# Attention scores as plain float32 products, two heads in turn on halves of the rows, in a banded attention with a GLU behind it

## The chip, the core and the metric

The kernel runs on one core of a Trainium2 chip. The metric is the device time of one execution in microseconds: the median of 3 runs before is 849.68 us (849.67 to 851.6). The engines are TensorE (PE in the rows; PEld is its weight load), VectorE (DVE), ScalarE (ACT), GpSimd (POOL) and SyncE (SP), which issues all DMAs here.

## The reference

There are 8 batches of 8 heads, 512 local tokens, 32 global tokens, head size 64. A local query sees the 32 global keys and the local keys at most 32 places away; a global query sees all 544 keys.

```python
k_all, v_all = concat(k_g, k_l), concat(v_g, v_l)
out_g = softmax(q_g @ k_all.T / 8) @ v_all
s_ll = where(|i - j| <= 32, q_l @ k_l.T / 8, -1e9)
out_l = softmax(concat(q_l @ k_g.T / 8, s_ll)) @ v_all
x = concat(out_g, out_l)                  # 4608 tokens x 512 (8 heads x 64)
out = ((x @ w1) * (x @ w2)) @ w3 @ w_out  # d_model 512, d_ff 1024
```

## The kernel before

Heads are taken one after the other (n = 0 to 63), the two heads of a pair (m = n // 2) share tiles. For each head the scores of a block of 128 queries against their window of keys (192 or 256 columns: 32 global keys and the band, `WIN`) are made by PE into the tile `s`, which has one buffer of two banks. DVE then scales, masks and takes the row's largest value in one pass per block (`minus_max`, line 550), written to one of two tiles P; ACT takes the exponential with its sum (line 554); PE transposes P (line 583), ACT and DVE copy that into the tiles PT and G, some edges go through DRAM (`gd`, `G<-gd`), and PE multiplies with the values (`av`, lines 659 and 665). Pairs are normalized with a reciprocal that goes through DRAM (`rd`, `R`). The 32 global queries have their own scores (`sg`), in the same buffer `s`.

The GLU is folded: w34 = w3 @ w_out is made on the chip in float32 (`fold`, line 950) while the weights arrive. Then every 256 tokens are multiplied with w1 and w2 (`first`, lines 816 to 818, tiles ap and bp), gated, and multiplied with w34 (`second`, lines 848 to 850, acc). These products are of type float32r: each operand is split into a high part of that type and the rest (low), and three products (high x high, high x low, low x high) are added.

Two ways of making scores stand side by side. Heads 0 to 15 (n < `NS`) use plain float32: one load of K and one of Q per pair, with the two heads on the partitions 0 to 63 and 64 to 127, and four products per head on that half of the rows (line 539); the trace has two records for each plain float32 product. Heads 16 to 63 use the split: K is loaded twice, on both halves, ACT rounds it to the high part (`kh`), POOL or DVE subtract (`kl`); Q becomes one tile with the high part on 64 partitions and the low part on the other 64 (`qs`); eight products per head on all 128 rows (line 546).

The order of the whole program is made before it runs. Each step has a cost per engine (`COST`) and a due number from the table `DUE`; `list_schedule` goes through simulated time, and on each free engine the ready step with the lowest due number begins. `take` and `read` add the waits for tiles with few buffers. All engines then run their steps in that fixed order. Seven `idle_products` open the program on PE: three on all rows, then four in turn on rows 0 to 63 and 64 to 127 (lines 390 to 396), on zeros.

Of the kernel before, what the change touches and what calls it, by code (L numbers as in the profile page):

```python
# [7 lines left out]
F32 = mybir.dt.float32  # L8
# [12 lines left out]
KD = 608  # L21
# [9 lines left out]
def i(ap):  # L31
# [3 lines left out]
NX, NO, NK, NQ, MA, NS = (5, 6), 3, 3, 2, 4, 16  # L35
# [10 lines left out]
    scores32=1650, values32=(1180, 1130), gscores32=930, take=(446, 521),  # L46
# [272 lines left out]
def band_attention_glu_kernel(  # L319
# [35 lines left out]


    cs = const.tile([128, 128 + 256 + 192], F32, tag="cs", name="cs")
    ident = cs[:, 0:128]
    mask = cs[:, 128:384]
    masks = [cs[:, 384:576], mask, mask, mask[:, 0:192]]  # L360
    Ps = [const.tile([128, PW], F32, tag=f"P{e}", name=f"P{e}") for e in range(2)]
    TT = const.tile([128, 2, 352], F32R, tag="TT", name="TT")
    vgs = const.tile([128, H, 2, 64], F32R, tag="vgs", name="vgs")
    xg = const.tile([128, NP, TG], F32, tag="xg", name="xg")
    sums = p1q.tile([128, 2, 2, 4], F32, tag="sums", name="sums")

    def view(ap, offset, *dims):
# [1109 lines left out]
```

## Time and profile before

| | us |
|---|---|
| median of 3 runs | 849.68 |
| span of the profiled execution | 848.0 |
| TensorE busy | 833.2 (98%) |
| VectorE busy | 567.0 (67%) |
| ScalarE busy | 536.0 (63%) |
| GpSimd busy | 383.4 (45%) |

The span runs from the first to the last instruction; launch and end lie outside it. Products on PE are pipelined: a row's duration is that of one record, and the next one may start before it ends, so what a product costs a busy PE is read from start to start.

### The profile page before, as it was taken

What the parts mean: (1) busy time and instruction counts of PE and PEld (TensorE: products, weight loads), DVE (VectorE), ACT (ScalarE), POOL (GpSimd) and SP (SyncE); (2) the same over time, 40 slices, a digit from 0 to 9 for tenths busy, and PEclk for the clock granted to TensorE, in tenths of its full rate; (3) what the DMA queues carried; (4) which work ended last, traced back from release to release, by engine and by line L of the source; (5) the groups of instructions that cost most, each with busy time, mean ns of one, the idle gap of its engine ahead of it and who ended that gap; (6) DMA issues with size and microseconds to landing.
All of it is one profiled execution on the core that took longest, in us unless ns stands there. A gap on an engine that the chain in (4) does not pass through costs nothing.

```text
span 848.0 us, 17752 instructions
## 1 busy us (share of the span) xinstructions
PE 833.2 (98%) x5818; PEld 750.2 (88%) x5818; DVE 567.0 (67%) x1499; ACT 536.0 (63%) x1445; POOL 383.4 (45%) x477
## 2 busy tenths in 40 slices
PE   7999999899999999999999999999999999999998
PEld 4756679799999999999999999999989999999997
DVE  5677777867777786877787767776877778531111
ACT  4666776765767786867666768676767767521111
POOL 1201455534638474747563645654755656310000
PEclk8999999999999999999999999999999999999999
DMA  9787656554647464746554554645555644200000
GB/s 292 228 250 229 183 165 165 144 129 104 147 94 170 114 158 109 170 104 165 114 137 118 131 142 121 140 116 143 123 136 123 146 97 117 50 26 2 26 18 33
DMA packets 194372, 109.75 MB, mean 129 GB/s; under 512 B 150056, under 2 KB 158504, under 8 KB 194280
## 3 DMA queue, kind: packets, MB, share of 16 engines
q1 hardware_dynamic: 194280, 108.61, 50.1%
q8 instruction: 46, 0.75, 0.4%
q14 instruction: 46, 0.38, 0.2%
HBM read 85.52 MB, written 20.28 MB: 125 GB/s over the span
## 4 chain that ended last, share of the span: by engine, by line
PE 75%; DMA 3%; SPq 1%; ACT 0%; issue 0%; POOL 0%; DVE 0%; ACTq 0%; POOLq 0%
PE acc L848 7%; PE acc L849 7%; PE ap L816 7%; PE acc L850 7%; PE bp L816 7%; PE bp L817 6%; PE ap L817 6%; PE bp L818 6%; PE ap L818 6%; PE av L665 5%; PE s L546 5%; PE t L583 3%; DMA G<-gd 2%; PE av L659 2%; PE sg L715 1%; PE s L539 1%
## 5 line engine op out<-in xcount | busy, mean ns | idle before, releaser
L816 PE MATMUL ap<-x,w12h 128*128 128x256 f32 x544 | 153.8, 283 | 0.0
L816 PE MATMUL bp<-x,w12h 128*128 128x256 f32 x544 | 153.0, 281 | 0.0
L817 PE MATMUL bp<-x,w12h 128*128 128x256 f32 x544 | 151.1, 278 | 0.0
L817 PE MATMUL ap<-x,w12h 128*128 128x256 f32 x544 | 151.0, 278 | 0.0
L818 PE MATMUL bp<-x,w12l 128*128 128x256 f32 x544 | 151.0, 278 | 0.0
L818 PE MATMUL ap<-x,w12l 128*128 128x256 f32 x544 | 150.9, 277 | 0.0
L554 ACT ACTIVATE P<-P,small 128x256 f32<-128x256 f32 (+1 forms) x256 | 121.5, 476 | 19.0 <-DVE small L550 18.7
L550 DVE CUSTOM_DVE_ANT_0 P<-s,cs 128x192 f32<-128x192 f32 (+1 forms) x256 | 88.3, 383 | 25.8 <-PE s L546 16.5
L816 PEld LDWEIGHTS ap<-x,w12h 128*128 128x128 f32 x544 | 102.3, 188 | 2.1 <-issue 0.4
L817 PEld LDWEIGHTS bp<-x,w12h 128*128 128x128 f32 x544 | 102.5, 188 | 1.1
L817 PEld LDWEIGHTS ap<-x,w12h 128*128 128x128 f32 x544 | 102.5, 188 | 1.1
L816 PEld LDWEIGHTS bp<-x,w12h 128*128 128x128 f32 x544 | 102.2, 188 | 1.4 <-issue 0.2
L818 PEld LDWEIGHTS bp<-x,w12l 128*128 128x128 f32 x544 | 102.6, 189 | 0.0
L818 PEld LDWEIGHTS ap<-x,w12l 128*128 128x128 f32 x544 | 102.4, 188 | 0.0
L679 DVE TENSOR_TENSOR u<-av,cb 64x352 f32<-64x352 f32 x112 | 57.5, 519 | 27.1 <-ACT cb L462 25.2
L465 POOL TENSOR_TENSOR kl<-kr,kh 128x608 fp32r<-128x608 f32 x37 | 56.5, 1527 | 36.9 <-ACT kh L462 26.6
L665 PE MATMUL av<-PT,vs 128*128 128x192 f32 x448 | 61.4, 263 | 0.0
L950 PE MATMUL w<-wo,w3f 128*128 128x512 f32 x128 | 60.2, 604 | 0.0
L462 ACT COPY cb<-av 64x352 f32<-64x352 f32 x93 | 41.6, 447 | 27.2 <-PE av L665 25.9
L665 PEld LDWEIGHTS av<-PT,vs 128*128 128x128 f32 x448 | 52.4, 162 | 0.7
L465 POOL TENSOR_TENSOR qs<-qr,qs 64x512 fp32r<-64x512 f32 x31 | 42.4, 1368 | 17.6 <-issue 9.3
L554 ACT ACTIVATION_READ_ACCUMULATOR P<-P,small 128x1 f32 x256 | 48.1, 188 | 0.0
(811 smaller groups left out, 2137.9 us busy)
## 6 DMA issues: line engine op xcount, KB each, us to landing
kr<-in_kd_t_dram SPq DMA_DIRECT2D x96, 152.0 KB, 3.0
raw_w<-in_w_t_dram SPq DMA_DIRECT2D x24, 512.0 KB, 4.9
kpr<-in_kp_t_dram SPq DMA_DIRECT2D x32, 272.0 KB, 3.2
out_dram<-o_None SPq DMA_DIRECT2D x33, 256.0 KB, 2.8
R<-rd SPq DMA_DIRECT2D x64, 128.0 KB, 3.2
gd<-TT SPq DMA_DIRECT2D x112, 64.0 KB, 2.7
vr<-in_v_t_dram SPq DMA_DIRECT2D x28, 256.0 KB, 3.2
G<-gd SPq DMA_DIRECT2D x112, 64.0 KB, 2.7
```

The source lines that it names most:

```text
L465: (eng or nc.gpsimd).tensor_sub(dst, src, f(hi))
L550: nc.vector.tensor_tensor_reduce(blk(n, e), T["st", n][:, e, 0 : WIN[e][1]], masks[e], -0.125, 3.0e38, ALU.add, ALU.min, T["mn", n][:, e : ...
L554: nc.scalar.activation(blk(n, e), blk(n, e), AF.Exp, bias=T["mn", n][:, e : e + 1], scale=-1.0, accum_out=T["sm", n // 2][:, n % 2, e : e ...
L665: nc.tensor.matmul(av[0:r, o : o + 32 * (s1 - s0)], v[:, 0:r], PT[:, s0:s1, y, j], start=False, stop=(j % 2 == 1 and (plain or y == 1)), s ...
L679: nc.vector.tensor_add(T["u", n // 2][r : r + 64, x], T.pop(("av", n, x))[r : r + 64, 0:352], T["cb", n][r : r + 64, x])
L816: nc.tensor.matmul(d, wh[:, k, c, :], x[:, 0, 0:w], start=(k == m % 2 == 0), stop=False, skip_group_check=True)
L817: nc.tensor.matmul(d, wh[:, k, c, :], x[:, 1, 0:w], start=False, stop=False, skip_group_check=True)
L818: nc.tensor.matmul(d, wl[:, k, c, :], x[:, 0, 0:w], start=False, stop=(k == 3), skip_group_check=True)
L848: nc.tensor.matmul(a, gh[:, m % 2, sl], wh[:, c], start=(m == 0), stop=False, **part)
L849: nc.tensor.matmul(a, gh[:, m % 2, sl], wl[:, c], start=False, stop=False, **part)
L850: nc.tensor.matmul(a, gl[:, m % 2, sl], wh[:, c], start=False, stop=(m in (5, 7)), **part)
L950: nc.tensor.matmul(T["w34", t], T["w3f", t, j // 4][:, j % 4], T["wo"][:, j], start=(j == 0), stop=(j == 7))
```

## The change

All 64 heads get their scores as plain float32 products. `scores(m, h)` makes half of the windows (e = 0, 1 or e = 2, 3) for both heads of a pair, the heads in turn, head 0 on rows 0 to 63 into one bank and head 1 on rows 64 to 127 into the other; so there are 64 score steps of four products with a planned cost of 872 ns instead of 16 of four with 1650 ns and 48 of eight with 897 ns. The split of K and Q, its loads and its steps go. P has three tiles. The table DUE has new numbers (its first line is shown). At the end of the program 22 products on the float32r weights are added, whose results nothing reads.

```diff
-NX, NO, NK, NQ, MA, NS = (5, 6), 3, 3, 2, 4, 16
+NX, NO, NK, NQ, MA, NP_ = (5, 6), 3, 3, 2, 4, 3
-    scores32=1650, values32=(1180, 1130), gscores32=930, take=(446, 521),
+    scores2=872, values32=(1180, 1130), gscores32=930, take=(446, 521),
 DUE = tuple(int(x) / 100 for x in """
-    3500 0 102500 2500 274500 5000 273000 1500 500 7500 7000 9500 6000 19500 19000 21000 9000 27500 28000 30000 13500 36500 36000 37000
+    47500 225000 87500 1382500 163000 1058500 371500 1268000 274500 1018000 1698500 664500 297000 700500 68000 337500 313500 366500 23000 1072000 865000 1788500 737500 787000
...
-    Ps = [const.tile([128, PW], F32, tag=f"P{e}", name=f"P{e}") for e in range(2)]
+    Ps = [const.tile([128, PW], F32, tag=f"P{e}", name=f"P{e}") for e in range(NP_)]
+    def trial_products():
+        a, b = (W12[m][0].rearrange("p a b c -> p (a b c)") for m in (0, 1))
+        o = [ps_1.tile([128, 512], F32, tag=t, name=f"trial_{t}") for t in ("t0", "t1", "a", "b")]
+        def product(at, st, mv, w=256, rows=(0, 128), cols=128, out=None):
+            r = slice(*rows)
+            d = o[at][0:cols, 0:w] if out is None else out
+            nc.tensor.matmul(d, b[r, st : st + cols], mv if mv is not None else a[r, st : st + w], start=True, stop=True,
+                             skip_group_check=True)
+        for j in range(3):
+            product(0, 128 * j, None)
+        for j in range(3):
+            product(0, 128 * j, None, rows=(0, 64))
+            product(1, 128 * j, None, rows=(64, 128))
+        for j in range(3):
+            product(2, 128 * j, None, cols=64)
+        for j in range(2):
+            product(3, 128 * j, view(a, 0, [2, 256]))
+        for j in range(2):
+            for r in range(4):
+                product(r, 128 * j, None, rows=(32 * r, 32 * r + 32))
...
-    def scores(n):
...
-        qs, kh, kl = T.pop(("qs", n)), T.pop(("kh", n)), T.pop(("kl", n))
-        for e in range(4):
+    def scores(m, h):
+        st = ps_1.tile([128, 2, 2, 256], F32, tag="s", name=f"s{m}_{h}")
...
+        q, k = T["q2", m], T["k2", m]
+        for e in (2 * h, 2 * h + 1):
             o, w = WIN[e]
-            for j, kk in enumerate((kh, kl)):
-                nc.tensor.matmul(st[:, e, 0:w], qs[:, 128 * e : 128 * e + 128], kk[:, o : o + w],
-                                 start=(j == e % 2 == 0), stop=(j == 1), skip_group_check=True)
+            for x in range(2):
+                r = slice(64 * x, 64 * x + 64)
+                nc.tensor.matmul(st[:, x, e % 2, 0:w], q[r, 128 * e : 128 * e + 128], k[r, o : o + w],
+                                 start=(e % 2 == 0), stop=True, skip_group_check=True)
...
-            if n + 1 < NH:
-                take("s", 1, ("s", n + 1), ("s", n + 1))
+            if n % 2 and n + 1 < NH:
+                for k in (("s", (n + 1) // 2, h) for h in range(2)):
+                    take("s", 1, k, k)
...
+        trial_products()
```

What the order of instructions shows. First PE in the steady part: before, head 32 is scored by one block between main products (kh and kl are the parts of K, qs those of Q).

```order
L817 MATMUL ap2_1_6_4834<-x2_3_1_3798,w12h6_999 128x256
L818 MATMUL ap2_1_6_4834<-x2_3_1_3798,w12l6_1000 128x256
L546 MATMUL s32_4856<-kh32_4776,qs32_4754 128x192
L546 MATMUL s32_4856<-kl32_4788,qs32_4754 128x192
L546 MATMUL s32_4856<-kh32_4776,qs32_4754 128x256
L546 MATMUL s32_4856<-kl32_4788,qs32_4754 128x256
L546 MATMUL s32_4856<-kh32_4776,qs32_4754 128x256
L546 MATMUL s32_4856<-kl32_4788,qs32_4754 128x256
L546 MATMUL s32_4856<-kh32_4776,qs32_4754 128x192
L546 MATMUL s32_4856<-kl32_4788,qs32_4754 128x192
L816 MATMUL bp2_1_6_4872<-x2_0_1_2782,w12h6_999 128x256
L817 MATMUL bp2_1_6_4872<-x2_0_1_2782,w12h6_999 128x256
```

Now the same pair (16) has two blocks on the undivided tiles kq and qp. The first:

```order
L798 MATMUL bp2_1_4_4483<-x2_3_1_3587,w12l5_1042 128x256
L526 MATMUL s16_0_4610<-kq16_3835,qp16_4119 128x192 x2
L526 MATMUL s16_0_4610<-kq16_3835,qp16_4119 128x256 x2
L796 MATMUL ap2_1_6_4617<-x2_0_1_2704,w12h6_1043 128x256
L797 MATMUL ap2_1_6_4617<-x2_0_1_2704,w12h6_1043 128x256
L798 MATMUL ap2_1_6_4617<-x2_0_1_2704,w12l6_1044 128x256
```

Between it and the second stand 36 main products:

```order
L797 MATMUL bp2_1_6_4638<-x2_3_1_3587,w12h7_1045 128x256
L798 MATMUL bp2_1_6_4638<-x2_3_1_3587,w12l7_1046 128x256
L526 MATMUL s16_1_4675<-kq16_3835,qp16_4119 128x256 x2
L526 MATMUL s16_1_4675<-kq16_3835,qp16_4119 128x192 x2
L639 MATMUL av0_31_4681<-G1_1103,vgs_83 128x288
L645 MATMUL av0_31_4681<-PT1_1059,vs15_4462 128x192
L645 MATMUL av0_31_4681<-PT1_1059,vs15_4462 64x192
```

The eight products of one head have become four, the first half of the windows of two heads, and the second half follows 36 products later.

Next PE at the start of the program: before, one head is scored ahead of the first fold and transposes (w34 is the fold, t a transpose, sg the scores of global queries).

```order
L707 MATMUL sg0_151<-kpr0_116,QG0_112 128x272 x2
L396 MATMUL idle0_102<-vgs_82 128x256 x2
L539 MATMUL s0_170<-kq0_129,qp0_127 128x192
L539 MATMUL s0_170<-kq0_129,qp0_127 128x256 x2
L539 MATMUL s0_170<-kq0_129,qp0_127 128x192
L707 MATMUL sg1_188<-kpr1_140,QG0_112 128x272 x2
L950 MATMUL w34_0_196<-wo_99,w3f0_0_146 128x512
L583 MATMUL t0_0_201<-cs_78,P0_79 128x128 x4
L588 MATMUL t1_0_202<-cs_78,P0_79 128x128 x3
```

Now both halves of pair 0 stand there in a row:

```order
L687 MATMUL sg0_155<-kpr0_128,QG0_113 128x272 x2
L386 MATMUL idle0_103<-vgs_83 128x256 x2
L526 MATMUL s0_0_168<-kq0_115,qp0_132 128x192 x2
L526 MATMUL s0_0_168<-kq0_115,qp0_132 128x256 x2
L526 MATMUL s0_1_181<-kq0_115,qp0_132 128x256 x2
L526 MATMUL s0_1_181<-kq0_115,qp0_132 128x192 x2
L687 MATMUL sg1_206<-kpr1_140,QG0_113 128x272 x2
L930 MATMUL w34_0_216<-wo_100,w3f0_0_187 128x512
L563 MATMUL t0_0_224<-cs_78,P0_79 128x128 x4
L568 MATMUL t1_0_225<-cs_78,P0_79 128x128 x3
```

and those of pair 1 a little later, with one fold between its second half and the transposes of its first head:

```order
L930 MATMUL w34_1_236<-wo_100,w3f1_0_213 128x512
L930 MATMUL w34_0_216<-wo_100,w3f0_0_187 128x512
L526 MATMUL s1_1_351<-kq1_195,qp1_144 128x256 x2
L526 MATMUL s1_1_351<-kq1_195,qp1_144 128x192 x2
L930 MATMUL w34_0_216<-wo_100,w3f0_1_336 128x512
L563 MATMUL t0_2_375<-cs_78,P2_81 128x128 x4
L568 MATMUL t1_2_376<-cs_78,P2_81 128x128 x3
L687 MATMUL sg2_390<-kpr2_165,QG0_113 128x272 x2
```

The second half of a pair, and with it four passes on DVE, has moved ahead of the first fold; head 1 is scored there too.

Last SP, which issues the loads: before, around heads 32 and 33 (kr is K on both halves, qr is Q, gd and G the edges by way of DRAM).

```order
L401 DMA qr32_4371<-in_q_t_dram 64x512
L611 DMA gd28_4377<-TT_81 128x4x32 x2
L605 DMA PT1_1050<-TT_81 32x2x96
L606 DMA PT1_1050<-TT_81 32x2x96
L419 DMA kr32_4419<-in_kd_t_dram 64x608
L420 DMA kr32_4419<-in_kd_t_dram 64x608
L431 DMA vr15_4433<-in_v_t_dram 128x512
L616 DMA G1_1045<-gd28_4377 32x16x32 x2
L419 DMA kr33_4461<-in_kd_t_dram 64x608
L420 DMA kr33_4461<-in_kd_t_dram 64x608
```

Now, around pair 16:

```order
L415 DMA qp15_3749<-in_q_t_dram 128x512
L438 DMA kpr15_3752<-in_kp_t_dram 128x544
L545 DMA rd13_3786<-sums_85 128x2x4
L591 DMA gd26_3802<-TT_82 128x4x32 x2
L421 DMA kq16_3835<-in_kd_t_dram 128x608
L585 DMA PT1_1059<-TT_82 32x2x96
L586 DMA PT1_1059<-TT_82 32x2x96
L596 DMA G1_1103<-gd26_3802 32x16x32 x2
```

Four K loads of a pair have become one (kq), and its two Q loads one (qp); the moves into PT, gd and G have fewer issues ahead of them.

## Rows read from the trace of the kernel before

**Rows 1.** The page: busy us (share) by engine, granted clock in 40 slices.

```profile
PE 833.2 (98%) x5818; PEld 750.2 (88%) x5818; DVE 567.0 (67%) x1499; ACT 536.0 (63%) x1445; POOL 383.4 (45%) x477
PEclk8999999999999999999999999999999999999999
```

**Rows 2.** Stretches: us, busy us (xinstructions) per engine, granted clock, DMA share, GB/s.

```profile
0.00:25.00 25.00, 19.13 (x68) 13.46 (x69) 14.34 (x42) 11.20 (x31) 4.18 (x9) 0.86 0.85 275
25.00:116.00 91.00, 91.00 (x335) 55.30 (x333) 66.00 (x178) 62.71 (x172) 21.43 (x26) 1.00 0.71 216
116.00:200.00 84.00, 81.23 (x572) 74.26 (x571) 63.90 (x177) 56.85 (x167) 45.47 (x63) 1.00 0.56 145
200.00:740.00 540.00, 537.66 (x4094) 509.59 (x4093) 399.51 (x1068) 384.14 (x1040) 308.55 (x376) 1.00 0.54 127
740.00:848.00 108.00, 104.21 (x757) 97.61 (x755) 23.26 (x37) 21.06 (x39) 3.80 (x6) 1.00 0.06 21
```

**Rows 3.** Waits of PE: total us, times, longest us.

```profile
PE s L539 <- DVE small L734: 3.4, 2, 1.9
PE av L659 <- DMA G<-gd: 2.4, 6, 0.8
PE sg L707 <- DMA kpr<-in_kp_t_dram: 2.0, 1, 2.0
```

**Rows 4.** Timeline of PE at 175 us: start us, us, line, operation.

```profile
175.04 0.28 PE L818 MATMUL bp<-x,w12l 128*128 128x256 f32 x1
175.24 1.78 PE L539 MATMUL s<-kq,qp 64*128 64x192 f32 x8
176.95 0.38 PE L816 MATMUL ap<-x,w12h 128*128 128x256 f32 x1
177.17 0.28 PE L817 MATMUL ap<-x,w12h 128*128 128x256 f32 x1
```

**Rows 5.** Timeline, two narrow windows of one plain block.

```profile
193.62 0.59 PE L539 MATMUL s<-kq,qp 64*128 64x256 f32 x2
...
194.49 0.48 PE L539 MATMUL s<-kq,qp 64*128 64x192 f32 x2
```

**Rows 6.** Timeline of PE at 285 us, around a block of split scores.

```profile
284.83 0.28 PE L817 MATMUL bp<-x,w12h 128*128 128x256 f32 x1
284.95 0.28 PE L818 MATMUL bp<-x,w12l 128*128 128x256 f32 x1
...
285.96 0.30 PE L816 MATMUL ap<-x,w12h 128*128 128x256 f32 x1
286.10 0.28 PE L817 MATMUL ap<-x,w12h 128*128 128x256 f32 x1
```

**Rows 7.** PE by shape until 6.2 us: xcount | busy us, mean ns.

```profile
L396 PE MATMUL idle<-vgs 128*128 128x256 f32 x6 | 2.9, 661 | 1.2 <-DVE vgs L393 1.2
L396 PE MATMUL idle<-vgs 64*128 64x256 f32 x8 | 2.0, 643 | 0.0
```

**Rows 8.** Groups by shape, ACT and POOL: passes over K.

```profile
L462 ACT CAST kh<-kr 128x608 fp32r<-128x608 f32 x48 | 33.5, 699 | 20.5 <-PE s L546 16.8 <-issue 2.2 <-POOL QG L465 1.5
...
L465 POOL TENSOR_TENSOR kl<-kr,kh 128x608 fp32r<-128x608 f32 x37 | 56.5, 1527 | 36.9 <-ACT kh L462 26.6 <-DVE small L550 3.2 <-PE av L659 2.7
```

**Rows 9.** Group by shape, DVE: the pass that reads the scores.

```profile
L550 DVE CUSTOM_DVE_ANT_0 P<-s,cs 128x256 f32<-128x256 f32 x128 | 49.9, 418 | 0.1
```

**Rows 10.** Timeline of PE, first 16 us; in brackets idle time and its releaser.

```profile
10.38 1.78 PE L539 MATMUL s<-kq,qp 64*128 64x192 f32 x8 [1.91 <-DVE small L734]
14.15 2.15 PE L707 MATMUL sg<-kpr,QG 128*128 128x272 f32 x4 [2.00 <-DMA kpr<-in_kp_t_dram]
```

**Rows 11.** Timeline of all engines, the last 4 us.

```profile
843.94 0.28 PE L850 MATMUL acc<-w34h,gl__11088 128*128 128x256 f32 x1
844.65 0.82 SPq L863 DMA_DIRECT2D out_dram<-o  x2
```

**Rows 12.** Stretches as above, records of line 539 alone (PE, then weight loads).

```profile
116.00:200.00 84.00, 11.58 (x53) 8.77 (x51) 1.00 0.56 145
```

More of the change, by code (lines that the diff above doesn't have):

```diff
@@ L396, in idle_products @@
             nc.tensor.matmul(T["idle"][r0 // 64][:, 0:w], z[r0:r1, 0:128], z[r0:r1, 0:w], start=True, stop=True)
-    def load_q(n):
-        b, h = divmod(n, H)
-        qr = p2.tile([128, 512], F32, tag="qr", name=f"qr{n}", bufs=NQ)[0:64]
-        nc.sync.dma_start(qr, q_t[b, h])
-        T["qr", n] = qr
+    def trial_products():
[18 more added lines that the diff above has]
+                product(r, 128 * j, None, rows=(32 * r, 32 * r + 32))
     def load_q2(m):
@@ L414, in load_k2 @@
         T["k2", m] = kr
-    def load_k(n):
-        b, h = divmod(n, H)
-        kr = p2.tile([128, KD], F32, tag="kr", name=f"kr{n}", bufs=NK)
-        nc.sync.dma_start(kr[0:64], kd_t[b, h])
-        nc.sync.dma_start(kr[64:128], kd_t[b, h])
-        T["kr", n] = kr
     def load_pair(n):
@@ L482, in prep_vg @@
             lo_of(vgs[0:64, :, 1, :], vgr, vgs[0:64, :, 0, :], eng)
-    def prep_k(n, part, eng=None):
-        if part == 0:
-            T["kh", n] = p1.tile([128, KD], F32R, tag="kh", name=f"kh{n}")
-            hi_of(T["kh", n], T["kr", n], eng)
-        else:
-            T["kl", n] = p1.tile([128, KD], F32R, tag="kl", name=f"kl{n}")
-            lo_of(T["kl", n], T.pop(("kr", n)), T["kh", n], eng)
-    def prep_q(n, part, eng=None):
-        if part == 0:
-            T["qs", n] = p1q.tile([128, 512], F32R, tag="qs", name=f"qs{n}")
-            hi_of(T["qs", n][0:64], T["qr", n], eng)
-        else:
-            qs = T["qs", n]
-            lo_of(qs[64:128], T.pop(("qr", n)), qs[0:64], eng)
     def prep_v(n, s, part, eng=None):
@@ L524, in blk @@
     def blk(n, e):
-        return Ps[n % 2][:, PAT[e] : PAT[e] + WIN[e][1]]
-    def scores(n):
-        st = ps_1.tile([128, 4, 256], F32, tag="s", name=f"s{n}")
-        T["st", n] = st
-        T["mn", n] = minima()[:, 4 * (n % 2) : 4 * (n % 2) + 4]
-        if n % 2 == 0:
-            T["sm", n // 2] = sums[:, n // 2 % 2]
-        if n < NS:
-            rows = slice(64 * (n % 2), 64 * (n % 2) + 64)
-            q, k = T["q2", n // 2][rows], T["k2", n // 2][rows]
-            for e in range(4):
-                o, w = WIN[e]
-                nc.tensor.matmul(st[:, e, 0:w], q[:, 128 * e : 128 * e + 128], k[:, o : o + w], start=(e % 2 == 0),
-                                 stop=True, skip_group_check=True)
-            return
-        qs, kh, kl = T.pop(("qs", n)), T.pop(("kh", n)), T.pop(("kl", n))
-        for e in range(4):
+        return Ps[n % NP_][:, PAT[e] : PAT[e] + WIN[e][1]]
+    def scores(m, h):
+        st = ps_1.tile([128, 2, 2, 256], F32, tag="s", name=f"s{m}_{h}")
+        for x in range(2):
+            T["st", 2 * m + x] = st
+        if h == 0:
+            T["sm", m] = sums[:, m % 2]
+            for x in range(2):
+                c = 4 * ((2 * m + x) % 2)
+                T["mn", 2 * m + x] = minima()[:, c : c + 4]
+        q, k = T["q2", m], T["k2", m]
+        for e in (2 * h, 2 * h + 1):
             o, w = WIN[e]
-            for j, kk in enumerate((kh, kl)):
-                nc.tensor.matmul(st[:, e, 0:w], qs[:, 128 * e : 128 * e + 128], kk[:, o : o + w],
-                                 start=(j == e % 2 == 0), stop=(j == 1), skip_group_check=True)
+            for x in range(2):
+                r = slice(64 * x, 64 * x + 64)
+                nc.tensor.matmul(st[:, x, e % 2, 0:w], q[r, 128 * e : 128 * e + 128], k[r, o : o + w],
+                                 start=(e % 2 == 0), stop=True, skip_group_check=True)
     def minus_max(n, e):
-        nc.vector.tensor_tensor_reduce(blk(n, e), T["st", n][:, e, 0 : WIN[e][1]], masks[e], -0.125, 3.0e38,
+        nc.vector.tensor_tensor_reduce(blk(n, e), T["st", n][:, n % 2, e % 2, 0 : WIN[e][1]], masks[e], -0.125, 3.0e38,
                                        ALU.add, ALU.min, T["mn", n][:, e : e + 1])
@@ L578, in transposes @@
     def transposes(n):
-        P = Ps[n % 2]
+        P = Ps[n % NP_]
         tt = [ps_1.tile([128, 4, 128], F32, tag=f"t{x}", name=f"t{x}_{n}") for x in range(2 if n < H else 1)]
@@ L590, in turn @@
     def turn(n):
-        P, raw = Ps[n % 2][:], f(TT[:, 1])
+        P, raw = Ps[n % NP_][:], f(TT[:, 1])
         nc.vector.transpose(view(raw, 0, [128, 3], [1, 96]), view(P, 160, [32, 3], [256, 3], [1, 32]))
@@ L1013, in tile_orders @@
         take("qr", NQ, ("q2", 0, "r"), ("load", "q2", 0))
-        for k in (("sg", 0), ("s", 0), ("sg", 1), ("tg", 0)):
+        for k in (("sg", 0), ("s", 0, 0), ("s", 0, 1), ("sg", 1), ("tg", 0)):
             take("s", 1, k, k)
@@ L1019, in tile_orders @@
         for n in range(NH):
-            if n + 2 < NS and n % 2 == 0:
+            if n + 2 < NH and n % 2 == 0:
                 take("kr", NK, ("k2", n // 2 + 1, "r"), ("load", "k2", n // 2 + 1))
                 take("qr", NQ, ("q2", n // 2 + 1, "r"), ("load", "q2", n // 2 + 1))
-            if NS <= n + 2 < NH:
-                take("kr", NK, ("k", n + 2, "r"), ("load", "k", n + 2))
-                take("qr", NQ, ("q", n + 2, "r"), ("load", "q", n + 2))
             if n + 2 < NH and (n + 2) % H == 0:
@@ L1043, in tile_orders @@
                         take("cb", 1, ("cg", k[1]), ("cg", k[1]))
-            take("P", 2, ("P", n), ("mmax", n, 0))
-            if n >= NS:
-                for tag in "kh", "kl", "qh":
-                    take(tag, 1, (tag, n), (tag, n))
+            take("P", NP_, ("P", n), ("mmax", n, 0))
     tile_orders()
@@ L1054, in head @@
         t = base(n) - 10.0
-        if n < NS:
-            if n % 2 == 0:
-                add(("load", "k2", n // 2), dma(380), t - 12, (), load_k2, n // 2, nbytes=128 * KD * 4)
-                add(("load", "q2", n // 2), dma(430), t - 12.1, (), load_q2, n // 2, nbytes=128 * 512 * 4)
-            read(("s", n), ("k2", n // 2, "r"), ("q2", n // 2, "r"))
-            add(("s", n), only("PE", COST["scores32"]), t + 2.7, [("load", "k2", n // 2), ("load", "q2", n // 2)], scores, n)
-        else:
-            add(("load", "k", n), dma(480, 590), t - 12, (), load_k, n, nbytes=2 * 64 * KD * 4)
-            add(("load", "q", n), dma(510), t - 12.1, (), load_q, n, nbytes=64 * 512 * 4)
-            for c, tag, due, fn in (("k", "kr", t - 2.0, prep_k), ("q", "qr", t - 1.2, prep_q)):
-                h, l = (c + "h", n), (c + "l", n)
-                add(h, hi(COST[c + "h"], 600 if c == "k" else 512), due, [("load", c, n)], fn, n, 0, eng=True)
-                add(l, either(c + "l"), due + 1.4, [h], fn, n, 1, eng=True)
-                read(h, (c, n, "r"))
-                read(l, (c, n, "r"), h)
-                read(("s", n), h)
-            read(("s", n), ("kl", n))
-            add(("s", n), only("PE", COST["scores"]), t + 2.7, [("kl", n), ("ql", n)], scores, n)
+        if n % 2 == 0:
+            m = n // 2
+            add(("load", "k2", m), dma(380), t - 12, (), load_k2, m, nbytes=128 * KD * 4)
+            add(("load", "q2", m), dma(430), t - 12.1, (), load_q2, m, nbytes=128 * 512 * 4)
+            for h in range(2):
+                me = ("s", m, h)
+                read(me, ("k2", m, "r"), ("q2", m, "r"))
+                add(me, only("PE", COST["scores2"]), t + 2.7 + 2.0 * h,
+                    [("load", "k2", m), ("load", "q2", m), *[("s", m, 0)] * h], scores, m, h)
         for e in range(4):
@@ L1075, in head @@
             add(("mmax", n, e), only("DVE", COST["mmax"][w]), t + 4.0 + 0.1 * e,
-                [("s", n), *([("mmax", n, e - 1)] if e else [("load", "cs")])], minus_max, n, e)
-            read(("mmax", n, e), ("s", n))
+                [("s", n // 2, e // 2), *([("mmax", n, e - 1)] if e else [("load", "cs")])], minus_max, n, e)
+            read(("mmax", n, e), ("s", n // 2, e // 2))
             add(("exps", n, e), only("ACT", COST["exps"][w]), t + 4.9 + 0.4 * e, [("mmax", n, e)], exps, n, e)
```

320 rows, old and new, of the table DUE are left out of this document.

## The prediction

> **What bounds the kernel now.** I read the page first. TensorE (PE) is busy for 833.2 of 848.0 us, and its clock is granted in full in every slice but the first [rows 1]. An average can hide a stage with another limit, so the table of stretches came next [rows 2]. PE is busy for 91.00 of 91 us, 81.23 of 84 and 537.66 of 540, and no other engine passes 78% of one of these stretches. PE idles in four places: 5.87 us in the first 25, 2.77 us up to 200, 2.34 us up to 740, and 3.79 us at the end, after its last product. The view of waits says what PE waited for: 3.4 us for the largest score of the global queries, 2.4 us for the transfer that fills G, 2.0 us for one early load [rows 3]. So the kernel's time is the sum of PE's starts. Work taken from ScalarE (ACT), VectorE (DVE) or GpSimd (POOL) can give back at most its part of 2.77 + 2.34 = 5.1 us. The question is what the new score products cost PE.
>
> **The price of the parts on PE.** I take prices from start to start, since the shown ends of products are modelled.
>
> A plain block of before (one head, four products, eight records on half the rows): the product ahead of it starts at 175.04, the second product behind it at 177.17. That is 2.13 us, less two ordinary starts of 0.11 [rows 4, 6]: 1.91 us. Inside it two 192-column records cost 0.16 us apiece (0.48 for two that overlap, less one record's 0.32) and 256-column ones 0.215 [rows 5], so the eight need 4 x 0.16 + 4 x 0.215 = 1.50 us. The other 0.41 us is fixed: 0.09 ahead of the block (0.20 from start to start instead of 0.11), 0.21 inside it (1.71 from 175.24 to 176.95, less 1.50) and 0.11 behind (0.22 from 176.95 to 177.17).
>
> A split block of before (one head, eight products on all rows): from 284.95 to 286.10, 1.15 us, less two starts of 0.115: 0.92 us [rows 6].
>
> A half block of after (two heads, two windows each, heads in turn on the halves) isn't in the trace as such. The nearest rows are the warm-up products. Three on all rows make six records and take 2.9 us; the four behind them, in turn on rows 0 to 63 and 64 to 127, make eight records and take 2.0 us [rows 7]. That is 0.97 us against 0.50 per product: two halves run side by side. They ran in the first stretch, where the granted clock is 0.86 on the mean [rows 2] and partly at the lower of its two levels (1.2 GHz); the score blocks will run at the upper (2.4), but only the ratio is used. A half block then streams like half a plain block, 0.75 us, and pays the fixed 0.41 once: 1.16 us. Bounds: 1.16 with full overlap, 1.91 with none; I take 1.16, since the warm-up rows are the same kind of product in the same turn. Nothing speaks for a price below it: every row range is entered and left.
>
> The fixed 0.41 us is also what the Trainium skill says: TensorEngine Tiling, Tiling Modes (Key Properties) states that a change of the tiling mode drains the TensorE. The trace agrees: 0.41 us for going in and out [rows 4]. The page's speedup of up to 2x for 64 rows leaves that drain out. By it alone a half block would be 0.75 us and the change worth 64 x 0.41 = 26 us more; the rows decide against it.
>
> **The sum.** Heads 0 to 15: 16 plain blocks become 16 half blocks, 16 x (1.16 - 1.91) = -12.0 us. Heads 16 to 63: 48 split blocks become 48 half blocks, 48 x (1.16 - 0.92) = +11.5 us. PE's own sum: -0.5 us. The change makes the scores of two batches cheaper and those of six dearer.
>
> **What goes from the other engines.** 48 heads lose four passes each, K and Q, high and low part: on ACT 0.70 us for each K, on POOL 1.53 us for most low parts [rows 8]. The K loads fall from two per head to one per pair, the Q loads from one per head to one per pair, so SP issues 96 DMAs fewer. All of this lies beside PE. It counts only in PE's 5.1 us of idle time from 25 to 740 us: G comes sooner when SP's queue is shorter and the parts ahead of it (edges, low parts) stand in shorter queues on ACT and POOL. I take two thirds: -3.3 us. Bounds: -5.1 (all of it goes) and +5 (new waits, next).
>
> **What is late next.** The score tile has one buffer, so a half block waits until DVE has read four blocks of the half ahead. Four passes at 0.42 us at most [rows 9] make 1.5 to 1.7 us, with what stands between them on DVE. In the steady part 21 to 36 products of 0.11 us stand between the halves (2.4 to 4 us), which covers that. In the first 40 us the cover is thin: the first two halves stand next to each other, and one fold product stands between the second half of pair 1 and the transposes that need its last two passes on DVE and their exponentials; the passes alone take as long as that product. There I count +0.5 us. The start has the other sign too: before, PE waits 1.91 us for the first block and 2.00 us for the second global product, and runs its four records in 2.15 us behind that [rows 10]; after, the second half fills part of the gap, but the keys of the first global product are issued behind two more loads. I count 0 for the start, from -2 to +2. The third P tile removes the wait of a pair's second head for the transposes of the head before; without it, scoring both heads at once would stall, so it has no gain of its own.
>
> The trial products are 22 PE instructions behind the last real one, on full, half, quarter rows and half columns. At 0.11 us each, and more for the strided ones and the switches, they take 2 to 3.5 us. PE's last product starts at 843.94, ACT empties it, and the last stores are issued from 844.65 and land before the span ends at 848.0 [rows 11]. These 3.8 us and more cover them. I count 0; the bound is +1.
>
> Total: -0.5 - 3.3 + 0.5 = -3.3 us on the 848.0 us of the profiled execution, which stands 1.7 us below the median of 849.68 (launch and end lie outside the span). Forecast: 849.7 - 3.3 = 846.4 us. A measurement of this kernel can tell about 0.3%, or 2.5 us, from no change, so this lies just beyond the edge.
>
> **Rivals.**
> (a) PE's idle time stays: -0.5 of products, waits exchanged one for one: 849 us. For it: the table shows PE hardly idle from 200 to 740 [rows 2], and the transfer of G takes the same path as before.
> (b) More goes than I count: all 5.1 us of idle time and 2 us of the start: 849.7 - 0.5 - 5.1 - 2 = 842 us. For it: the parts of K and Q go in six of the eight batches, and every queue beside PE gets shorter. Against: G's wait is a transfer's latency.
> (c) Slower, by the weights: up to 116 us PE folds weights that arrive by DMA, with the DMA engines busy 71 to 85% [rows 2]. If they set the pace, the gain of the plain blocks there is lost. Of the 128 records of plain blocks 53 lie behind 116 us [rows 12], 6.6 blocks, so 9.4 x 0.75 = 7 us would be gone and the +11.5 us stay: 849.7 - 0.5 + 7 - 3.3 + 0.5 = 853.4 us. It decides if PE is seen waiting for raw weights before 116 us. Against: PE waits for none of them now [rows 3].
> (d) Slower, the halves don't overlap in full: a half block halfway between the bounds, 1.53 us, costs 64 x 0.37 = 24 us more (870 us), one of 1.91 us 48 us more (894 us). In a sentence of its own: TensorE: Matmul & The Clock Gate, Part 3 of the Trainium skill has four row tiles at 3.07x instead of 4x; at that share of the ideal the streaming part would be 0.98 us, an estimate, and the kernel some 862 us. Against: the warm-up rows show 1.95 times [rows 7].
>
> **How the numbers follow.** Forecast 44%, own range 844 to 849; (a) 26%; (b) 12%; (c) 13%; (d) 5%. Faster by over 0.3% (under 847.1): two thirds of the forecast's share, 0.29, plus (b) 0.12 and 0.03 of (a): 0.44. Slower (over 852.2): (c), (d) and 0.01 of (a): 0.19. Within: 0.37. The range of 8 in 10 leaves out (d), a third of (b) and a part of (c): 840.5 to 854 us.
>
> **What would show it.** A half block between main products, start to start, at 1.1 to 1.2 us, with records of two heads starting in pairs; 64 blocks at 1.5 us or more would be (d). PE idle from 25 to 740 us at 2 to 3 us instead of 5.1, with "DVE small" and "DMA G" smaller in the view of waits; if it is 5 or more, (a). Waits for raw weights before 116 us: (c). The last store landing about 3.7 us after PE's last real product, with the trial products inside that time. The prediction is wrong if the fixed 0.41 us differs when two row groups enter together, 0.1 us of which makes 6.4 us, or if the first 40 us are off by more than 2 us.

## The result, and the profile after

The changed kernel takes 854.7 us (median, 854.25 to 855.09), the kernel before 849.7 on the same chip: a ratio of 1.0061, interval 1.0043 to 1.0078. The forecast was 846.4 us, with a range up to 854. It went the other way and fell just outside.

The page of the changed kernel, busy time by engine and the granted clock in 40 slices:

```profile
PE 836.9 (98%) x5840; PEld 732.5 (86%) x5840; DVE 529.1 (62%) x1456; ACT 480.5 (56%) x1341; POOL 292.1 (34%) x432
PEclk8999999999999999999999999999999999999999
```

Against [rows 1], ACT lost 55 us of work, POOL 91 and DVE 38; PE gained 3.7, and the span grew from 848.0 to 853.2 us. The table of stretches tells where (columns as in [rows 2]):

```profile
0.00:25.00 25.00, 17.54 (x73) 11.34 (x73) 14.33 (x43) 11.12 (x32) 4.04 (x9) 0.86 0.88 290
25.00:116.00 91.00, 90.73 (x357) 53.95 (x356) 68.12 (x184) 64.69 (x174) 28.23 (x35) 1.00 0.71 217
116.00:200.00 84.00, 76.80 (x573) 70.47 (x572) 63.31 (x164) 53.76 (x157) 42.72 (x66) 0.98 0.61 144
200.00:740.00 540.00, 540.00 (x4026) 492.42 (x4025) 357.59 (x1026) 328.26 (x937) 214.08 (x318) 1.00 0.47 112
```

PE's idle time, stretch by stretch, before against after: 5.87 and 7.46 us; 0 and 0.27; 2.77 and 7.20; 2.34 and 0.00. From 200 us on PE never waits any more, but between 116 and 200 it waits 4.4 us longer. The view of waits of PE (total us, times, longest us) names the largest:

```profile
PE av L639 <- DMA G<-gd: 3.1, 1, 3.1
PE s L526 <- DVE small L714: 3.0, 2, 2.5
PE sg L687 <- DVE small L530: 1.6, 2, 1.5
PE s L526 <- issue: 1.5, 1, 1.5
```

The first is head 8, the first of batch 1. PE's timeline around it, and the granted clock of the 3.2 us behind it (columns of the stretches):

```profile
124.30 0.28 PE L798 MATMUL ap<-x,w12l 128*128 128x256 f32 x1
127.67 0.37 PE L639 MATMUL av<-G,vgs 128*128 128x288 f32 x1 [3.10 <-DMA G<-gd]
...
129.35 0.41 PE L798 MATMUL ap<-x,w12l 128*128 128x256 f32 x1
129.56 0.41 PE L796 MATMUL ap<-x,w12h 128*128 128x256 f32 x1
129.77 0.41 PE L797 MATMUL ap<-x,w12h 128*128 128x256 f32 x1
```

```profile
128.80:132.00 3.20, 3.20 (x17) 3.20 (x16) 2.59 (x6) 2.38 (x9) 2.37 (x3) 0.50 0.53 170
```

Products that follow each other at 0.11 us just before the wait follow at 0.21 behind it, where the granted clock is 0.50, the lower of its two levels (1.2 GHz). Together the wait and this stretch cost 3.1 + 3.2 x 0.5 = 4.7 us.

The forecast's main price, a half block of scores, is read between main products as before:

```profile
379.65 0.28 PE L798 MATMUL bp<-x,w12l 128*128 128x256 f32 x1
379.86 1.03 PE L526 MATMUL s<-kq,qp 64*128 64x192 f32 x8
380.82 0.39 PE L796 MATMUL ap<-x,w12h 128*128 128x256 f32 x1
381.04 0.28 PE L797 MATMUL ap<-x,w12h 128*128 128x256 f32 x1
```

From 379.65 to 381.04 are 1.39 us; less two starts of 0.115 that leaves 1.16 us, as forecast. The 17 half blocks of this trace that stand between gate products with no wait all cost 1.163 or 1.164 us, by the gate's common distance of 0.113.

To place the 5.2 us I took the distance from each PE product's start to the next one's, set it against the usual distance of its shape, and added up what is over (113 ns for the 256-column products of the gate, ap and bp in the rows). PE's last real product starts at 843.94 us before and at 849.21 after, 5.3 us later:

| part of PE's time, us | before | after | difference |
|---|---|---|---|
| score blocks, with going in and out | 75.3 | 74.05 | -1.25 |
| waits | 12.5 | 15.3 | +2.8 |
| gate products beyond 113 ns (the half clock among them) | 9.4 | 12.2 | +2.8 |
| all else | | | +0.9 |

### The profile page after: what moved, and what is told of

It reads as the page before. It is cut to its first block, busy times and chain, and to the rows that moved or that the text cites. A ratio compares the mean times of both kernels' runs of the same rounds, so it can differ in the third digit from the quotient of the medians.

```text
span 853.2 us, 17309 instructions
## 1 busy us (share of the span) xinstructions
PE 836.9 (98%) x5840; PEld 732.5 (86%) x5840; DVE 529.1 (62%) x1456; ACT 480.5 (56%) x1341; POOL 292.1 (34%) x432
## 4 chain that ended last, share of the span: by engine, by line
PE 96%; DMA 1%; DVE 1%; issue 1%; SPq 0%; ACT 0%; POOL 0%; DVEq 0%; ACTq 0%
PE acc L828 8%; PE bp L796 8%; PE ap L796 8%; PE acc L830 7%; PE s L526 7%; PE acc L829 7%; PE bp L797 7%; PE ap L797 7%; PE bp L798 7%; PE ap L798 7%; PE av L645 7%; PE w L930 6%; PE t L563 3%; PE av L639 3%; PE sg L695 2%; DMA raw_w12s<-in_w_t_dram 1%
## 5 line engine op out<-in xcount | busy, mean ns | idle before, releaser
L534 ACT ACTIVATE P<-P,small 128x192 f32<-128x192 f32 (+1 forms) x256 | 121.5, 476 | 49.6 <-DVE small L530 49.2
L530 DVE CUSTOM_DVE_ANT_0 P<-s,cs 128x256 f32<-128x256 f32 (+1 forms) x256 | 87.5, 384 | 39.4 <-PE s L526 37.0
L526 PE MATMUL s<-kq,qp 64*128 64x256 f32 (+1 forms) x512 | 66.3, 378 | 5.9 <-DVE small L714 3.0
L526 PEld LDWEIGHTS s<-kq,qp 64*128 64x128 f32 x512 | 42.4, 187 | 22.4 <-issue 8.5
L466 DVE TENSOR_TENSOR PT<-t,PT 128x512 fp32r<-128x512 f32 x56 | 38.5, 687 | 23.5 <-ACT PT L463 22.8
```

Of the source, the lines that this page charges most:

```text
L526: nc.tensor.matmul(st[:, x, e % 2, 0:w], q[r, 128 * e : 128 * e + 128], k[r, o : o + w], start=(e % 2 == 0), stop=True, skip_group_check=True)
L530: nc.vector.tensor_tensor_reduce(blk(n, e), T["st", n][:, n % 2, e % 2, 0 : WIN[e][1]], masks[e], -0.125, 3.0e38, ALU.add, ALU.min, T["mn" ...
L534: nc.scalar.activation(blk(n, e), blk(n, e), AF.Exp, bias=T["mn", n][:, e : e + 1], scale=-1.0, accum_out=T["sm", n // 2][:, n % 2, e : e ...
```

## The experiments

Four theories stood. A: the prices hold everywhere, the cheap early blocks bring 12 us and the dear late ones take 11; what tipped the balance are waits of this order of steps. B: the making of the weights sets the pace of the first 116 us, and cheap early scores only turn into waits. C: only the order is at fault; it is planned with 0.87 us per half block (`scores2=872`) where the chip takes 1.16. D: a wait that is removed only gives way to the next one.

To compare parts under equally good orders, several kernels replace the planner's loop by a written order. It was found by shifting steps in the engines' queues while adding up the measured prices:

```diff
-        for _, n, e in list_schedule(steps, after, held):
+        for n, e in SEQ:
```

In before_front, after_front, early_pairs and early_pairs_2 this covers only the steps of the first 235 us; behind them each kernel keeps its own order (the two early kernels that of before). In q_b, q_late and q_a the whole order is new. The kernels with one part of the change choose by head (q_late: n >= 16):

```diff
+def PAIR(n):
+    return n < 16
...
-        if n < NS:
+        if PAIR(n):
```

**Whole orders anew: q_b (kernel before), q_late (late pairs alone), q_a (the whole change).** The counterpart of q_late, the early pairs alone with the third P tile (q_early), has no time: beside the split's tiles it needs 32 KB per partition for a pool where 28.6 are left. early_pairs below takes its place with two P tiles.

> The kernel before with nothing changed but the order of its steps, found anew in the same way with the measured prices; the yardstick for the other three. If the order of before was as good as can be: 849 to 850. By the waits that its trace shows (the TensorE idle 5.9 us in the first 25 us, 2.8 and 2.3 later) an order can give back at most about 10 us: 840 to 850 under every theory.

> The other part alone: heads 0 to 15 plain one head at a time, as in the kernel before, heads 16 to 63 as paired half blocks without the split of K and Q, third P tile, no trial products, order found anew. Theory A: 48 x (1.16 - 0.92) = 11.5 us above the reordered kernel before, less up to 2.3 us of the idle time that the split's own waits left there: +9 to +11.5. Theory that the removed split work on ACT, DVE and POOL pays for the dearer products: 0 to +3. Theory C (the order table alone): 0 or below.

> The whole change with an order found anew, with 1.16 us per half block in place of the planned 0.87; trial products as in the change. Theory A: the sum of the two parts, -12 + 9 to 11.5, so 3 us below to 1 us above the reordered kernel before; against the changed kernel itself lower by what its waits between 100 and 200 us and at the start cost, some 5 to 10 us. Theory C (only the order is at fault, the prices are not): more than 5 us below the reordered kernel before. Theory B: 9 to 12 us above the reordered kernel before.

(In q_a's order one sum of head 22 is written before the sums of heads 18 and 19 have left their columns, so its result is not that of the reference; its PE products are as many as those of the changed kernel, 5840. Its time is used with this reserve.)

Measured: q_b 852.2 us (1.0049, 1.0032 to 1.0066), q_late 856.2 (1.0096, 1.0077 to 1.0115), q_a 848.8 (1.0011, 0.9997 to 1.0025). The yardstick itself came out slower than the kernel before, which no theory had expected: its waits fell by 2.9 us, but its gate products took 5.9 us more (last section). Between q_b and q_late the time rose by 4 us, less than half of A's +9 to +11.5. The score blocks took what A says: 74.96 us in q_b, 85.5 in q_late (+10.5), 73.1 in q_a (-12.4 against q_late). What was lost in late pairs came back as 1.7 us of waits and 4.7 us of gate products. q_a makes no difference to the kernel before. Against q_b, by which the theories were put, it is 0.0038 or 3.2 us lower, give or take some 1.9: at the edge of A's range (3 below to 1 above), short of C's 5 below, far from B's 9 to 12 above.

**The first 235 us anew: before_front, early_pairs, after_front.**

> The yardstick: the kernel before, with the order of the steps of its first 235 us written out anew in the same way, and its own order from there. The waits that its trace shows there (5.9 us in the first 25 us, 2.8 between 116 and 200) bound what an order can give: 842 to 849 us under every theory; the run with the whole order anew had 0.2 us of waits between 116 and 200 where before had 2.8, and lost it again behind 200.

> The early part of the change alone: heads 0 to 15 as paired half blocks, heads 16 to 63 with the split of K and Q as before; two P tiles as before (a third does not fit beside the split's tiles), no trial products. The order of the steps of the first 235 us is written out anew with the measured prices (half block 1.16 us, plain block 1.91), the rest keeps the order of the kernel before. Theory A (prices and place: early blocks gain 0.75 each and this gain arrives at the end if no wait eats it; late ones cost 0.24 each): 16 x 0.75 = 12 us below the kernel before_front, within 3, so about 836 to 840 us. Theory B (the weights' making and the loads set the pace of the first 116 us): within 3 us of before_front. Theory C (only the order table was at fault): says nothing here beyond B.

> The changed kernel with all its half blocks and trial products, the order of the steps of its first 235 us written out anew with 1.16 us per half block, its own order from there. Theory A: the 7.2 us of waits between 100 and 200 us and the products at half the clock behind them go, and what went wrong at the start, some 4 to 8 us: 847 to 851; not below before_front, because the late half blocks keep their 11 us. Theory C (only the order is at fault): 5 us or more below before_front.

Measured: before_front 843.8 us (0.9941, 0.9926 to 0.9956), early_pairs 836.0 (0.9847, 0.9832 to 0.9861), after_front 848.75 (1.0003, 0.9991 to 1.0015). Stretches of before_front, early_pairs and after_front from 116 to 200 us, in this order:

```profile
116.00:200.00 84.00, 84.00 (x606) 77.80 (x605) 66.44 (x190) 51.42 (x149) 44.20 (x73) 1.00 0.60 151
```

```profile
116.00:200.00 84.00, 83.72 (x642) 77.63 (x641) 68.74 (x195) 57.30 (x163) 50.44 (x74) 1.00 0.59 141
```

```profile
116.00:200.00 84.00, 80.95 (x606) 73.27 (x605) 66.93 (x188) 51.82 (x151) 36.74 (x63) 1.00 0.55 136
```

The waits between 116 and 200 us are a matter of order: 0 in before_front, 3.05 us in after_front where the changed kernel has 7.20, and the clock stays at its upper level. after_front lies 0.0062 or 5.3 us above before_front, where C wanted at least 5 below: C is out as the only cause. It is 0.0058 or 4.9 us below the changed kernel, as A has it. Its order gives more than that: the last 4548 products on PE stand in the same order in both, and after_front begins them at 229.8 us, 10.4 us sooner than the changed kernel (240.2), but takes 615.6 us for them in place of 611.4 (the paces of the gate products, below). The early pairs gain 7.8 us against before_front, short of A's 12 and far from B's 3. PE's own sum has all of it (score blocks 75.0 us in before_front, 62.8 in early_pairs, -12.2). Most of the missing 4 us went into the wait of one product, the second one for the global queries, which waits 2.0 us in before_front; the granted clock of the first 25 us is lower too, 0.80 against 0.93, and how much that took is not separated. In the view of PE's waits of early_pairs:

```profile
PE sg L706 <- DMA kpr<-in_kp_t_dram: 5.1, 1, 5.1
```

SP's queue in the first microseconds shows why (start, us, line, transfer), and its own view of waits what held it:

```profile
4.14 0.43 SPq L913 DMA_DIRECT2D raw_w<-in_w_t_dram  x1
9.25 0.65 SPq L427 DMA_DIRECT2D PT<-in_vg_t_dram  x1
9.94 0.59 SPq L913 DMA_DIRECT2D raw_wo<-in_wo_t_dram  x1
10.58 0.43 SPq L913 DMA_DIRECT2D raw_w<-in_w_t_dram  x1
11.05 0.43 SPq L418 DMA_DIRECT2D kpr<-in_kp_t_dram  x1
```

```profile
SPq L427 <- POOL PT L365: 4.7, 1, 4.7
```

The load into PT waits for a memset of PT, which POOL did behind a memset of vgs that in turn waited for the warm-up products to read vgs. Three loads and the second keys stood behind it, 4.6 us later than in the next kernel.

**That wait removed: early_pairs_2.** The order of the first 235 us is written out anew once more, on all engines; the part that is aimed at the wait:

```
 order on POOL:  clear QG,
-                clear vgs, clear G, clear PT
+                clear PT, clear G, clear vgs
```

> The kernel early_pairs with the order of its first 235 us written out once more: its 5.2 us wait of the TensorE at 11.3 us came from the load of V's global rows, which stood in SP's queue from 4.6 to 9.25 us for a memset of PT that POOL did after one of vgs, and held the second block of K behind it. Here the memset of PT goes first and vgs last. Theory A (what early_pairs missed of its 12 us was that wait): 3 to 5 us below early_pairs, 831 to 833. If the start is bound by something else (the landing of the first loads, the making of the first weights): within 1 us of early_pairs, 835 to 837.

Measured: 833.65 us (0.9828, 0.9809 to 0.9847). PT's load now stands at 4.62 and the second keys at 6.42 in SP's queue:

```profile
4.62 0.65 SPq L427 DMA_DIRECT2D PT<-in_vg_t_dram  x1
...
6.42 0.53 SPq L418 DMA_DIRECT2D kpr<-in_kp_t_dram  x1
```

```profile
0.00:25.00 25.00, 19.87 (x78) 12.64 (x79) 12.85 (x42) 12.06 (x32) 3.63 (x8) 0.86 0.79 254
25.00:116.00 91.00, 91.00 (x383) 56.46 (x382) 74.67 (x205) 62.87 (x173) 29.25 (x42) 1.00 0.78 238
116.00:200.00 84.00, 83.42 (x635) 77.22 (x634) 70.32 (x198) 55.30 (x155) 42.84 (x73) 1.00 0.59 145
```

PE is busy for 91.00 of 91 us while the weights are made, with scores 12 us cheaper: B is out. By the ratios early_pairs_2 is 0.0113 below before_front, 9.6 us of A's 12, and 0.0019 or 1.6 us below early_pairs, less than the 3 to 5 expected and not clear of the noise, some 2 us (a 2.2 us wait of the same product for DVE is left). As the whole early order is new, this difference is not the price of that one wait. It beats both kernels, by 1.7% and, through the kernel before, 2.3%. The step from it to after_front, whose 48 late heads are paired too and which keeps the changed kernel's order behind 235 us, is 0.0175 or 15 us; the score blocks are 11.3 us of that (62.5 and 73.8), the gate products 6, and the other parts take 2 back.

**One chain alone: batch1_sooner.** The changed kernel, with

```diff
+        order = [(n, e) for _, n, e in list_schedule(steps, after, held)]
+        for key, mark in ((("hi", 8, 5), ("vh", 4, 1)), (("hi", 8, 4), ("hi", 8, 5)), (("mi", 8), ("clear", "G", 1))):
+            at = {steps[n][0]: x for x, (n, _) in enumerate(order)}
+            order.insert(at[mark] + 1, order.pop(at[key]))
```

> The changed kernel with three steps of head 8 (the first of batch 1) issued earlier and nothing else: its two global weight pieces go to ACT ahead of the x casts that wait for the inverses, and the DMA G<-gd goes to the queue ahead of two weight fetches and two other transfers. The TensorE waited 3.1 us for that DMA at 124.3 us and then ran its next 3 us of products at 0.21 us in place of 0.11. Theory A (the early gain is lost to this chain): the wait shrinks to under 1 us, the half-clock products go, and since the TensorE is busy without a gap from 200 us on, the end comes 3 to 5 us sooner: 850 to 852. Theory D (a wait there only gives way to the next one, at 150 and 158 us): within 1 us of the changed kernel.

Measured: 854.2 us (1.0073, 1.0046 to 1.0101), no difference to the changed kernel. The edit did less than it was meant to: the G transfer passed the transfer of the edges, but not the weight fetches, since POOL's memset of G, which it now follows, comes late in the order. SP's queue and PE's wait in this run:

```profile
120.15 0.42 SPq L894 DMA_DIRECT2D raw_w12s<-in_w_t_dram  x1
120.66 0.91 SPq L596 DMA_DIRECT2D G<-gd  x2
121.62 0.69 SPq L585 DMA_DIRECT2D PT<-TT  x1
```

```profile
PE av L639 <- DMA G<-gd: 1.9, 1, 1.9
```

The transfer is issued at 120.66 instead of 122.73, PE waits 1.9 us instead of 3.1, and no stretch at the lower clock follows (granted clock 1.00 from 128.8 to 132). By 157 us PE is 3.0 us ahead of the changed kernel, 0.5 of them from before this wait. The same transposes in this run and in the changed kernel:

```profile
154.44 0.60 PE L563 MATMUL t<-cs,P 128*128 128x128 f32 x4
```

```profile
157.43 0.60 PE L563 MATMUL t<-cs,P 128*128 128x128 f32 x4
```

Behind them PE waits 2.48 us for the largest score of the global queries (2.47 in the changed kernel), and in this run it is that wait which the lower clock follows:

```profile
158.80:162.00 3.20, 3.20 (x18) 3.20 (x17) 3.10 (x16) 2.29 (x8) 1.60 (x2) 0.50 0.08 20
```

That takes 1.6 us back, and the span is 851.8 us against 853.2. So up to 157 us the chain is worth what A says, and half of that is lost at the next wait, which is D's kind of loss, by the clock and not by a longer wait. The 1.4 us left are less than the runs' spread, so the times of this test decide nothing; after_front's do.

**The trial products: no_trial.** `-        trial_products()`

> The changed kernel without its trial products at the end, and nothing else. If they are hidden behind the eviction and the last store (its trace has them from 849.2 to 851.8 us, with the last store ending the span at 853.2): no difference to the changed kernel, whose ratio to the kernel before was 1.0061. If they hold the end back: up to 2.6 us less, a ratio of 1.003.

Measured: 1.0079 (1.0048 to 1.0110) against 1.0061 with them: hidden, as the forecast had it. From the start of PE's last real product to the end of the span are 4.0 us in either trace (847.99 to 852.0, 849.21 to 853.2).

**The turn of the heads: not_in_turn.** One run.

```diff
-        for e in (2 * h, 2 * h + 1):
-            for x in range(2):
+        for x in range(2):
+            for e in (2 * h, 2 * h + 1):
```

> The changed kernel with the two heads of a half block one after the other instead of in turn: both blocks of the first head, then both of the second, so that neighbouring products use the same half of the rows. If the two halves overlap because products on different rows stand next to each other: only the two in the middle still do, and each half block takes some 0.35 us more for the products left alone (two of 192 or 256 columns in two passes, 0.16 and 0.21 us each by the distances between the plain kernel's records): 64 x 0.35 = 20 to 25 us slower, 870 to 880. If the order within a half block is nothing to the overlap (the engine pairs them in any order): 854.

Measured: 855.9 us, and the block costs the same. The first branch of the forecast is a plain miss, the second holds:

```profile
380.35 0.28 PE L798 MATMUL bp<-x,w12l 128*128 128x256 f32 x1
380.56 1.03 PE L526 MATMUL s<-kq,qp 64*128 64x192 f32 x8
381.53 0.39 PE L796 MATMUL ap<-x,w12h 128*128 128x256 f32 x1
381.75 0.28 PE L797 MATMUL ap<-x,w12h 128*128 128x256 f32 x1
```

From 380.35 to 381.75 are 1.40 us, where the turn by turn kernel has 1.39. The first records of both heads start 14 ns apart:

```profile
380.56 0.44 PE L526 MATMUL s<-kq,qp 64*128 64x192 f32 x2
```

The records don't name the head, but two records on one half start 0.16 us apart or more [rows 5]. So these two are the 192-column products of the two heads, although by the edit the first head's 256-column product stands between them.

**What makes the gate products slow: shift_all, shift_early.** One run each.

```diff
-IDLE = {None: ((0, 128, 256), (0, 128, 256), (0, 128, 256),
+IDLE = {None: ((0, 128, 256), (0, 128, 256), (0, 128, 256), (0, 128, 256),
```

> after_front with one more warm-up product (256 columns, all rows) at the start, and nothing else. It asks what makes the 256-column products of the two gate layers follow each other at 113 ns in some stretches and at 118 ns in others (73% of them at 116 ns or more in after_front, 43% in the changed kernel, 29 to 31% in before, before_front and early_pairs; 10.9 us against 5.3 us over 113 ns each). If it is where the instructions stand in TensorE's program, shifting all of them by one product changes the share by more than 15 points, and the time by some us. If it is the order of the work around them: the share stays at 70 to 76%, and the time within 1 us of after_front.

> early_pairs_2 with one more warm-up product at the start, and nothing else: the same question at the other end (28% at 116 ns or more). If the place of the instructions decides it, the share changes by more than 15 points; if the order of the work, it stays at 25 to 32% and the time at 832 to 835.

Measured: shares of 74% and 30%, with 850.7 and 833.35 us (the kernel before took 845.9 beside them). A shift of all products by one place changes nothing in the shares. (shift_all's time is 2 us from after_front's where 1 was named, on a single run.) But the order of the work doesn't decide it either: of the last 4548 products on PE, which stand in the same order in the changed kernel and in after_front, 40% of the gate's distances are at 116 ns or more in the one and 74% in the other. What decides it is open.

## Why the prediction was wrong

- **Bound by PE.** Right. From 200 us on the changed kernel's PE is busy for all 540 of 540 us, and what the other engines lost is worth nothing there.
- **Price of a half block, 1.16 us.** Right to 0.01, with both halves side by side and the fixed part paid once. Sum of the score blocks: -0.5 us forecast, -1.25 measured. Part by part: -12.0 forecast and -12.2 to -12.4 measured for the early ones, +11.5 and +10.5 to +11.3 for the late. Rival (d) falls.
- **PE's idle time from 25 to 740 us: "I take two thirds: -3.3 us".** This step failed (two thirds of 5.1 are 3.4, which changes nothing). The 2.34 us from 200 to 740 did go, but the 2.77 before them became 7.20 and 0.27 came ahead of 116: 5.11 us became 7.47, +2.4 in place of -3.3. The step's bound of +5 had room for new waits, its middle had none. And it had left the clock out: behind the 3.1 us wait 3.2 us of products ran at the lower level, 1.6 us more. With the first 25 us, idle time up to 740 us went from 11.0 to 14.9, +3.9 where the forecast's terms have -3.3 + 0.5. (The table above counts from start to start and has 2.8 of this under waits.)
- **Why it failed.** I asked which waits the removed work would end, not when PE would now arrive at those that stay. By 112 us PE was 4.8 us ahead of the kernel before, with the same products done: head 7's values start at 112.07 against 116.85. Head 8's G, which hangs on memsets, edges, the round through DRAM and SP's queue, came at about the same time as before: it is issued at 122.73 against 123.58, and its first product starts at 127.67 against 128.60. PE's lead turned into a wait there. Before, then after:

```profile
116.85 0.75 PE L659 MATMUL av<-G,PT 128*128 128x288 f32 x2
123.58 1.29 SPq L616 DMA_DIRECT2D G<-gd  x2
128.60 0.37 PE L659 MATMUL av<-G,vgs 128*128 128x288 f32 x1 [0.25 <-DMA G<-gd]
```

```profile
112.07 0.65 PE L639 MATMUL av<-G,PT 128*128 128x288 f32 x2
122.73 1.11 SPq L596 DMA_DIRECT2D G<-gd  x2
```

  The order that gets more out of it exists (after_front, early_pairs_2), but not in the table that came with the change.
- **The start, 0 from -2 to +2.** PE's idle time in the first 25 us grew by 1.6 us, against 0 and the +0.5 for the thin cover: within the bounds, on the dear side.
- **Trial products, 0.** Right.
- **Third P tile: without it scoring both heads at once would stall.** Not so for heads 0 to 15: early_pairs and early_pairs_2 have paired blocks and two P tiles, and PE is busy for 91.00 of the 91 us up to 116 us. For the late heads it wasn't tried.
- **Not forecast:** the gate products, some 1.2 us beyond the half clock here but 6 us between other kernels.
- **The rivals.** (a)'s sign came, 5 us or more of idle time from 25 to 740 us, but the waits weren't exchanged one for one, and its 849 us is 5.7 too low. (c) gave 853.4 us, the nearest number, but not for its reason: PE waits 0.27 us between 25 and 116 us. Its point, an early gain lost to something other than PE, was the right one, in the wrong place: the change of batch at 124 us. So its number is near by luck. (In (d), the estimate of 862 us comes to 861 by its own terms.)

## What to carry to other kernels

A gain on the engine that bounds a kernel reaches the end only if no other chain sets the pace further on: look for the next chain of transfers that doesn't move with the engine, and forecast the wait that the lead becomes there (and, where the trace shows one, the stretch at the lower clock behind it). A change that makes one stage cheaper and another dearer is two changes; price both, and take only the one that pays: here the pairs for heads 0 to 15 alone, 1.7% faster than before, 0.6% of which the new early order gives by itself (before_front). When a wait of an engine is removed, read what stands at the head of the queue that it waited for; one transfer that waits for a memset held four others.

## What the runs showed of the hardware that was not expected

- **Two row halves go on independently.** In not_in_turn the second head's first product starts 14 ns after the first head's, ahead of a product that stands before it in the program. The Trainium skill (TensorE: Matmul & The Clock Gate, Part 3, The mechanism) states that matmuls start and end strictly in program order. In this run the starts of products on different rows are not in that order, and the measurement decides; the shown ends are modelled and say nothing on it.
- **The lower clock behind a wait is not a matter of its length alone.** In the changed kernel it follows the wait of 3.1 us at 124 us and not that of 2.47 us at 158; in batch1_sooner it follows the same wait of 2.48 us at 155 and not that of 1.9 us at 124. Each time the stretch at the granted clock 0.50 takes some 1.6 us.
- **The same product at two paces.** 256-column products of the gate follow each other at 113 ns in some stretches and at 118 in others, at a granted clock of 1.00. The timeline of PE at 760 us, in the kernel before and in q_b:

```profile
760.12 0.28 PE L816 MATMUL ap<-x,w12h 128*128 128x256 f32 x1
...
760.46 0.28 PE L816 MATMUL bp<-x,w12h 128*128 128x256 f32 x1
```

```profile
760.09 0.28 PE L794 MATMUL bp<-x,w12h 128*128 128x256 f32 x1
...
760.44 0.28 PE L794 MATMUL ap<-x,w12h 128*128 128x256 f32 x1
```

  Three distances (the two products between are not shown) take 0.34 us in the first and 0.35 in the second; over some 3000 such products the share at 116 ns or more is 31% before, 43% in the changed kernel, 73% in q_b and in after_front, 28% in early_pairs_2. That is 5 to 11 us per run, as much as the whole effect of the change. Every stretch behind a 512-column product starts slow, and some change to the faster pace after about five products: in the longer stretches behind 140 us the sixth distance is still slow in 17% of them before, in 13% in the changed kernel and in 62% in after_front. Neither the order of the products on PE nor a shift by one place decides it, as shown above. What does is not settled.
